# Choosing the tokens of three sequences before the spectra of all eight are done, in a one-core spectral filter with routed experts

## The chip, the cores and the metric

One core of one Trainium2 chip runs the kernel. The metric is device microseconds for one execution. Engines are named as in the profile: PE (TensorE matmuls), PEld (weight loads), DVE (VectorE), ACT (ScalarE), POOL (GpSimd), SP (SyncE, here a queue of transfers).

## The reference

```python
# x (8, 2496, 256); filt_r, filt_i (1249, 256); capacity 80; 8 experts
X = np.fft.rfft(x, axis=1)
y = np.fft.irfft(X * (filt_r + 1j*filt_i)[None], n=2496, axis=1)   # (8, 2496, 256)
t = y.reshape(19968, 256)
logits = t @ w_gate                                   # (19968, 8)
expert_idx = argmax(logits, 1); gate_w = softmax(logits)[expert_idx]
out = 0
for e in range(8):                                    # 80 tokens of the largest gate_w each
    tok = the 80 tokens of expert e with the largest gate_w
    out[tok] = gate_w[tok, None] * (relu(t[tok] @ w1[e]) @ w2[e])
```

Only 640 of 19,968 rows of the filtered sequence are needed, but which ones is known only when all logits are.

## The kernel before

**Forward part.** The transform is split into 39 x 64 points. The work of sequence `b` is in 10 units `u`; a step `v` (line 482) takes unit `v`, `v = 10 b + u`, and issues, in an order written out by hand: `stage2` (PE tile `pb`, then two DVE multiplications by the filter, line 306, and two POOL additions, line 312), `transpose1` of unit `v+2` (tile `pt`), one or two `stage1` matmul groups of a later sequence (tile `pa`; they run out at step 67), and `turn` of unit `v-2` (tile `py`: the spectrum turned back and multiplied by the gate's columns; ACT copies the spectrum, line 333, DVE adds the gate part to `z`, lines 336 and 340). `pb`, `pt` and `pa` share the four one-bank buffers of the PSUM pool `fps`. Spectra 0 and 1 stay in SBUF, the others are stored to `yf` from ACT's queue.

**Logits and gating.** `logits` and the six parts of `gating` (softmax, best expert, each sequence's eight best candidates per row of 128) follow in the steps of the next pair of sequences; those of the last pair, 6 and 7, come after step 81 (lines 513 to 516).

**Choice.** `pick` (line 539) is a chain on DVE with small matmuls between: merge candidates (547, 549), ten rounds of maximum and replace over 256 values for the 80th best of each expert (563, 565), broadcast it (573), mark and count what is kept (580 to 591), pack codes (594 to 613), and two sets of one-hot matrices (628, 654) whose matmuls (633, 659) give the list of positions `idxb` of each sequence and the tokens of each expert.

**Back part.** Eight tiles, one a sequence (`back`, line 698): POOL gathers 128 rows of a cosine table by `idxb` (706), PE transposes them in five groups of four (715), DVE and ACT copy (718), 20 matmuls with the sequence's spectrum add up 128 filtered rows (721), which SP stores to `y_sel` (726).

**Branch and experts.** Line 759 reads a flag on every engine; were it set (a limit of the choice overrun), a general path would redo the choice. Then eight experts: gather 80 rows (785), transpose (795), two layers (802, 816), scatter (820). From the branch on, and in `pick` and `back`, the framework's scheduler orders the instructions; the forward part is in program order. The loads of zeros into `out`, spectra and weights are on SP's queue.

Of the kernel before, what the change touches and what calls it, by code (L numbers as in the profile page):

```python
# [10 lines left out]
AL = mybir.AluOpType  # L11
# [70 lines left out]
def kernel(  # L82
# [98 lines left out]
    NY = 2  # L181
    yf = {b: dpool.tile([128, NS, C], F32, name=f"yf_{b}") for b in range(NY, B)}
# [4 lines left out]
    ZR = S // 4  # L187
    zero_t = zp.tile([128, ZR * C // 128], F32, name="zero_t")
    zeros = list(range(4 * B))
# [8 lines left out]

    zs = [consts.tile([128, E, SP], F32, name=f"z_{i}") for i in range(2)]
# [3 lines left out]
    with ExitStack() as fctx:  # L203
        def pool(name, bufs, space=None):
            kw = {} if space is None else {"space": space}
            return fctx.enter_context(tc.tile_pool(name=name, bufs=bufs, **kw))

        tpool = pool("tables", 1)
# [3 lines left out]
        t2pool = pool("t2", 5)  # L212
        fspool = pool("fs", 3)
        ppool = pool("pp", 2)
        gpool = pool("gp", 1)
        fps = pool("fps", 4, PSUM)
        yps = pool("yps", 2, PSUM)

# [27 lines left out]
        def turn_filter(v, k):  # L246
            f = fst[:, v]
            ps = fps.tile([128, 2, NDB, 128], F32, name=f"pf_{k}_{v}", tag="f")
# [8 lines left out]
        def load_x(b, ch):  # L257
            xt = xpool.tile([NJ * N1, JC, C], F32, name=f"x_{b}_{ch}", tag="x")
            ng = min(JC, NG - JC * ch)
            nc.sync.dma_start(  # L260
                out=xt[:, 0:ng, :],
                in_=bass.AP(tensor=x.tensor, offset=x.offset + (b * S + JC * ch) * C,
                            ap=[[N2 * C, N1], [(NG - 1) * C, NJ], [C, ng], [1, C]]))
            st["x", b, ch] = xt

        def stage1(b, k):
# [4 lines left out]
            for i in range(2):  # L271
                for cb in range(NDB):
                    nc.tensor.matmul(  # L273
                        out=ps[:, i, :, 2 * NS * cb:2 * NS * cb + 2 * NS],
                        lhsT=xt[:, (2 * k + i) % JC, 128 * cb:128 * cb + 128],
# [40 lines left out]
        def turn(b, u):  # L316
# [17 lines left out]
            if b >= NY and u % 2 == 1:  # L334
                nc.scalar.dma_start(out=yf[b][:, 2 * u - 2:2 * u + 2, :], in_=st["ys"])
# [6 lines left out]
        def logits(b, part):  # L342
            if part == 0:
# [3 lines left out]
                ps = fps.tile([128, 2, 2, N2], F32, name=f"pv_{b}", tag="f")  # L347
# [6 lines left out]
            else:  # L354
                p, v = b // 2, st.pop(("v", b // 2))
                ps = fps.tile([128, 2, N1, 4], F32, name=f"pl_{p}", tag="f")
# [9 lines left out]
        def gating(p, part):  # L366
# [45 lines left out]
            elif part == 4:  # L412
                pk = fps.tile([128, 4, 2, N2], F32, name=f"pk_{p}", tag="f")
# [5 lines left out]
            else:  # L419
                for i in range(2):  # L420
# [6 lines left out]
                    scalar=16.0, in1=cbase[:, 2 * p:2 * p + 2, :], op0=AL.mult, op1=AL.add)  # L427

        LATE, LEAD = 2, 2
        with tc.manual_schedule():  # L430
# [50 lines left out]
            load_d(4)  # L481
            for v in range(B * NU + LATE):
                b, u = divmod(v, NU)
                if b < B:
# [16 lines left out]
                    if b > 0 and u in (2, 4, 6, 8):  # L501
                        put_zeros(1)
# [9 lines left out]
            assert not (xs or s1)  # L512
# [5 lines left out]
    wpool = ctx.enter_context(tc.tile_pool(name="weights", bufs=2))  # L518
    w1s, w2s = {}, {}

    def load_weights(e, wpool=wpool):
        w1s[e] = wpool.tile([128, NDB, FF], F32, name=f"w1_{e}", tag="w1")
        nc.sync.dma_start(out=w1s[e], in_=moe_w1[e].rearrange("(k p) f -> p k f", p=128))
        w2s[e] = wpool.tile([128, NFC, C], F32, name=f"w2_{e}", tag="w2")
        nc.sync.dma_start(out=w2s[e], in_=moe_w2[e].rearrange("(k p) d -> p k d", p=128))

    idxs = consts.tile([cap, E], I32, name="idxs")
    idxg = consts.tile([cap, E], I32, name="idxg")
    gate = consts.tile([cap, E], F32, name="gate")
    idxt = consts.tile([cap, E], I32, name="idxt")  # L530
    idxb = consts.tile([128, B], I32, name="idxb")
    more = consts.tile([1, 1], I32, name="more")
    nof = consts.tile([cap, E], F32, name="nof")
    ohb = consts.tile([cap, E, B], F32, name="ohb")
    bad = consts.tile([1, 1], I32, name="bad")
    y_sel = dpool.tile([128 * (B + NX), C], F32, name="y_sel")
    rows = rows_dram.ap()

    def pick(sp, pp):
        f_t = sp.tile([128, 4, KR], F32, name="f_t")  # L540
        off_e = sp.tile([128, 1], F32, name="off_e")

        row = sp.tile([128, KR], F32, name="row")
        rest = sp.tile([128, B * KC], F32, name="rest")
        cf = cand[:].rearrange("p b k -> p (b k)")
        for i in range(KR // 8):
            nc.vector.max(out=row[:, 8 * i:8 * i + 8], in_=cf if i == 0 else rest[:])
            if i + 1 < KR // 8:
                nc.vector.match_replace(out=rest[:], in_to_replace=row[:, 8 * i:8 * i + 8],
                                        in_values=cf if i == 0 else rest[:], imm_value=-1.0)  # L550
        spread = sp.tile([128, 16, KR], F32, name="spread")
        nc.vector.tensor_tensor(
            out=spread[:], in0=row[:].unsqueeze(1).to_broadcast([128, 16, KR]),
            in1=thot[:].unsqueeze(2).to_broadcast([128, 16, KR]), op=AL.mult)
        pall = pp.tile([E, 16 * KR], F32, name="pall")
# [684 lines left out]
```

## Time and profile before

| | us |
|---|---|
| three runs, median (lowest, highest) | 515.06 (513.83, 516.34) |
| the profiled execution, its own time | 514.17 |
| its span, first to last instruction | 512.3 |
| PE busy, share of the span | 441.4, 86% |
| DVE, ACT, POOL busy | 208.2, 204.0, 175.9 |
| mean granted TensorE clock | 0.925 of full speed |

A row of the page or of an answer gives an engine, the line of the kernel, the operation, `out<-in`, the sizes and times. Busy time tells little by itself here: the span falls into stages, and what ends the wait in a stage is read from that stage's rows.

### The profile page before, as it was taken

To read this page: it belongs to the slowest core of one execution; us is meant where nothing else is said; L and a number is where in the kernel's file an instruction comes from. 1 tells how busy PE (TensorE), PEld (TensorE's weight loads), DVE (VectorE), ACT (ScalarE), POOL (GpSimd) and SP (SyncE) were. 2 spreads that over 40 slices of the span, in tenths; PEclk is the share of its full clock that TensorE was granted. 3 is DMA by queue.
4 is the path that set the end of the run, shared out by engine and by line. 5 is a ranking of instruction groups with operands and counts; after the bars stand their busy time and mean duration, and the time that the engine had idled before them with its cause. 6 is when DMAs were issued, how large, how long until landed. Compare 5 with 4: busy or idle time off the path is not lost. (4 is left out here: it accounts for less than half of the span.)

```text
span 512.3 us, 8535 instructions
## 1 busy us (share of the span) xinstructions
PE 441.4 (86%) x3341; PEld 413.0 (81%) x3341; DVE 208.2 (41%) x552; ACT 204.0 (40%) x307; POOL 175.9 (34%) x244
## 2 busy tenths in 40 slices
PE   5789999999999999999999610299999992799993
PEld 5779999999999999999999500288888881788882
DVE  2145444448644477444697478312221110001110
ACT  4756766667666667766655210001100000001110
POOL 7586443434534335344356301520010002112111
PEclk9999999999999999999999955589999997569998
DMA  7999445458677676799223498533589913925830
GB/s 220 253 276 345 139 124 177 144 170 265 213 260 252 204 236 210 231 366 377 84 85 124 149 391 323 206 103 124 166 354 368 354 42 127 355 63 175 275 96 13
DMA packets 32849, 108.09 MB, mean 211 GB/s; under 512 B 3778, under 2 KB 13826, under 8 KB 31010
## 3 DMA queue, kind: packets, MB, share of 16 engines
q1 hardware_dynamic: 24656, 76.93, 45.5%
q0 software_dynamic: 3408, 14.74, 8.4%
q10 hardware_dynamic: 4738, 15.80, 7.8%
q8 instruction: 29, 0.48, 0.4%
q14 instruction: 18, 0.15, 0.1%
HBM read 68.97 MB, written 38.48 MB: 210 GB/s over the span
## 5 line engine op out<-in xcount | busy, mean ns | idle before, releaser
L312 POOL TENSOR_TENSOR p<-p,p 128x256 f32<-128x256 f32 x160 | 113.9, 733 | 133.1 <-DVE p L306 88.4
L306 DVE TENSOR_TENSOR p<-pb,ft 128x512 f32<-128x512 f32 x160 | 102.2, 680 | 9.8 <-PE pb L298 9.8
L273 PE MATMUL pa<-wf_t,x 117*128 117x120 f32 x704 | 91.9, 278 | 6.8 <-DMA x<-in_x_dram 6.8
L279 ACT COPY t<-pa 128x480 f32<-128x480 f32 x88 | 86.8, 1002 | 24.7 <-PE pa L273 24.4
L273 PEld LDWEIGHTS pa<-wf_t,x 117*128 117x128 f32 x704 | 86.0, 195 | 7.1 <-DMA x<-in_x_dram 5.4
L321 PE MATMUL py<-gi,p 128*128 128x136 f32 x640 | 88.1, 280 | 0.8 <-POOL p L312 0.8
L298 PE MATMUL pb<-d_t,t 128*128 128x128 f32 x640 | 84.4, 275 | 0.0
L321 PEld LDWEIGHTS py<-gi,p 128*128 128x128 f32 x640 | 79.8, 190 | 1.4 <-POOL p L312 1.4
L298 PEld LDWEIGHTS pb<-d_t,t 128*128 128x128 f32 x640 | 78.1, 192 | 0.0
L289 ACT COPY t<-pt 128x512 f32<-128x512 f32 x80 | 46.8, 585 | 63.8 <-PE pt L287 63.8
L336 DVE COPY z<-py 128x16 f32<-128x16 f32 x80 | 14.9, 186 | 100.9 <-ACT ysp L333 66.8
L721 PE MATMUL pr<-yb,wt 128*128 128x256 f32 x240 | 53.8, 379 | 0.0
L718 ACT COPY wt<-pw 128x512 f32<-128x512 f32 x16 | 9.4, 586 | 108.6 <-PE pw L715 108.6
L721 PEld LDWEIGHTS pr<-yb,wt 128*128 128x128 f32 x240 | 44.7, 190 | 5.6
L287 PE MATMUL pt<-ident,t 128*128 128x128 f32 x320 | 48.0, 273 | 0.0
L333 ACT COPY ysp<-py 128x512 f32<-128x512 f32 x60 | 35.3, 588 | 8.2 <-PE py L321 8.2
L287 PEld LDWEIGHTS pt<-ident,t 128*128 128x128 f32 x320 | 37.7, 141 | 0.0
L802 PEld LDWEIGHTS ph<-xs,w 128*128 128x128 f32 x256 | 36.1, 227 | 1.1 <-DVE xs L798 0.5
L802 PE MATMUL ph<-xs,w 128*128 128x80 f32 x256 | 36.1, 311 | 0.3 <-DVE xs L798 0.3
L715 PE MATMUL pw<-ident,gt 128*128 128x128 f32 x160 | 24.4, 297 | 11.3 <-DMA gt<-rows_tbl,idxb 8.5
L715 PEld LDWEIGHTS pw<-ident,gt 128*128 128x128 f32 x160 | 19.4, 151 | 16.7 <-issue 8.8
L816 PE MATMUL po<-w,hT 128*80 128x256 f32 x128 | 31.1, 393 | 0.0
(161 smaller groups left out, 299.5 us busy)
## 6 DMA issues: line engine op xcount, KB each, us to landing
out_dram<-zero_t SPq DMA_DIRECT2D x32, 624.0 KB
x<-in_x_dram SPq DMA_DIRECT2D x40, 468.0 KB
w<-in_moe_w_dram SPq DMA_DIRECT2D x16, 1024.0 KB
yf<-ysp ACTq DMA_DIRECT2D x30, 512.0 KB
yb<-yf SPq DMA_DIRECT2D x6, 2560.0 KB
x<-in_x_dram SPq DMA_DIRECT2D x8, 234.0 KB
d_t<-d_tbl SPq DMA_DIRECT2D x5, 256.0 KB
y_sel<-yr SPq DMA_DIRECT2D x8, 128.0 KB
```

Of the source, the lines that this page charges most:

```text
L273: nc.tensor.matmul(out=ps[:, i, :, 2 * NS * cb:2 * NS * cb + 2 * NS], lhsT=xt[:, (2 * k + i) % JC, 128 * cb:128 * cb + 128], rhs=wf_t[:], ...
L279: nc.scalar.copy(out=t1[:, 2 * k - h:2 * k - h + 2], in_=ps[:])
L287: nc.tensor.transpose(ps[:, i, cb, :], t1[:, a:a + 2, :].rearrange("p r n -> p (r n)"), ident[:])
L289: nc.scalar.copy(out=t2[:].rearrange("p i c -> p (i c)"), in_=ps[:].rearrange("p i c q -> p (i c q)"))
L298: nc.tensor.matmul(out=ps[:, cb, i], rhs=d_t[:, 2 * u + i, :], start=True, stop=True, lhsT=t2[:, i, 128 * cb:128 * cb + 128])
L306: nc.vector.tensor_tensor(out=pt, in0=ps[:].rearrange("p c s r q -> p (c s) r q"), in1=f.unsqueeze(2).to_broadcast([128, 2 * NDB, 2, NQ]), ...
L312: nc.gpsimd.tensor_tensor(out=yt[:, :, r, :], in0=yt[:, :, r, :], in1=pr[1][:, :, 1 - r, :], op=op)
L321: nc.tensor.matmul(out=ps[:, i, ZW * cb:ZW * cb + ZW], rhs=gi[:, cb, :], lhsT=yt[:, 2 * cb + i].rearrange("p r q -> p (r q)"), start=True, ...
L333: nc.scalar.copy(out=dst, in_=ps[:, :, E:E + C])
L715: nc.tensor.transpose(ps[:, i, :], gt[:, 128 * s:128 * s + 128], ident[:])
L721: nc.tensor.matmul(po[:], lhsT=wts[s // SG][:, s % SG, :], rhs=yb[:, s, :], start=(start and s == 0), stop=(stop and s == NS - 1))
L802: nc.tensor.matmul(ph[:, fc // 4, fc % 4, 0:cap], lhsT=w1s[e][:, k, 128 * fc:128 * fc + 128], rhs=xs[:, k, :], start=(k == 0), stop=(k == ...
```

## The change

1. **Early choice.** In steps 67 to 77 a first choice runs over the candidates of sequences 0 to 5 that are known by then. It finds for each expert a lower bound of the final threshold (the 80th best of 128 values, found from the other end by stripping the 48 smallest in six rounds), keeps what lies above it in sequences 0 to 2, and writes their `idxb`; `fetch(0)` and `fetch(1)` gather their table rows on POOL in steps 76 and 77. The gating parts of pair 4 and 5 are drawn together into steps 64 to 67 for it.
2. **Three tiles beside the end.** The back tiles of sequences 0 to 2 are cut into pieces (`turn_rows`: four transposes and an ACT copy; `add_rows`: four of the 20 matmuls) and put by hand between the matmuls of the last logits, gating and final choice, which gives `idxb` of sequences 3 to 7 and the tokens of all experts. All of it, tiles and experts included, is now in program order.
3. **PSUM and SBUF.** `fps` has three buffers (four before); one new bank `pkps` takes the filter transposes, logits, gating and choice. `t2` has four buffers (five before). All eight spectra are stored to `yf` (ten more transfers of 512 KB), zeros go out as 64 transfers of half the size, one a step.
4. **General path at the end.** The flag is read, and the branch taken or not, after the experts; the general path has experts of its own. While the flag is set, the experts before it write nothing.

```diff
-        t2pool = pool("t2", 5)
-        fps = pool("fps", 4, PSUM)
+        t2pool = pool("t2", 4)
+        sp = pool("pick", 1)
+        fps = pool("fps", 3, PSUM)
         yps = pool("yps", 2, PSUM)
+        pkps = pool("pkps", 1, PSUM)
...
+            early = {67: [lambda: pick_edge(0, 6, 8, -1.0)],
+                     68: [lambda: pick_all(0, 8)],
+                     70: [lambda: pick_least(0, 8 * n0 - 1, -1.0)],
+                     71: [lambda: pick_tau(0), lambda: pick_kept(0, 0, NE)],
+                     72: [lambda: pick_sums(0, 0, NE), lambda: pick_codes(0, 0, NE)],
+                     73: [lambda: pick_fields(0), lambda: pick_rows(0, 0, NE, 0),
+                          lambda: pick_rows(0, 0, NE, 1), lambda: pick_full(0, 0, NE)],
+                     74: [lambda: pick_rows(0, 0, NE, 2), lambda: pick_rows(0, 0, NE, 3)],
+                     75: [lambda: pick_rows(0, 0, NE, 4)],
+                     76: [lambda: pick_rows(0, 0, NE, 5), lambda: pick_rows(0, 0, NE, 6),
+                          lambda: fetch(0)],
+                     77: [lambda: fetch(1)]}
...
-                    if b > 0 and u in (2, 4, 6, 8):
+                    if b > 0:
                         put_zeros(1)
...
-                    if u in (4, 5, 6, 7, 8, 9):
+                    if b < 6 and u in (4, 5, 6, 7, 8, 9):
                         gating(b // 2 - 1, u - 4)
+                    elif b == 6 and u in (4, 5):
+                        gating(2, 2 * u - 8)
+                        gating(2, 2 * u - 7)
+                    elif b == 6 and u in (6, 7):
+                        gating(2, u - 2)
+                for act in early.pop(v, []):
+                    act()
+                if v >= B * NU:
+                    turn_rows(0, v - B * NU)
...
+            go(1)
             logits(B - 1, 0)
+            go(1)
             logits(B - 1, 1)
-            for part in range(6):
+            for part in range(4):
                 gating(NP - 1, part)
+            go(4)
+            gating(NP - 1, 4)
+            gating(NP - 1, 5)
+            bctx.close()
...
+            spectrum(2)
+            go(3)
+            pick_edge(1, B, KR, 1.0)
+            pick_all(1, KR)
+            for i in range(ntop):
+                pick_top(1, i, ntop, 16 * KR)
+            go(8)
+            fetch(2)
+            pick_least(1, cap - 1, 1.0)
+            pick_tau(1)
+            pick_kept(1, 0, B)
+            go(1)
+            pick_sums(1, NE, B)
+            pick_codes(1, NE, B)
+            pick_full(1, NE, B)
+            pick_bad()
+            pick_fields(1)
+            pick_slots(1)
+            for part in range(5):
+                pick_rows(1, NE, B, part)
+            pick_slots(0)
+            go(2)
+            pick_rows(1, NE, B, 5)
+            pick_rows(1, NE, B, 6)
+            for t in range(NE, 6):
+                fetch(t)
+            go(1)
+            pick_slots(2)
+            go(next(i for i, w in enumerate(work) if w[1] == NE))
+            go(len(work))
+            ex = Experts(nc, cap, ident, fp, ...)
...
+            ex.layer1(0)
+            for e in range(E):
+                if e + 3 < E:
+                    ex.gather(e + 3)
+                if e + 1 < E:
+                    ex.layer1(e + 1)
+                ex.layer2(e)
```

`go(n)` issues the next `n` pieces of the tiles, in the order add 0, turn 2, add 1, turn 3 and so on.

PE at the end of the forward part, from the last `pb` on. Before:

```order
L298 MATMUL pb_9_3184<-d_t,t_7_9_3152 128x128 x4
L321 MATMUL py_7_3195<-gi,p_7_7_3141 128x136 x4
L321 MATMUL py_8_3204<-gi,p_7_8_3168 128x136 x4
L321 MATMUL py_9_3213<-gi,p_7_9_3189 128x136 x4
L349 MATMUL pv_3222<-e_t,z_132 128x128 x2
L359 MATMUL pl_3226<-wi_t,v_3021 128x156 x4
L415 MATMUL pk_3250<-ident,key 128x128 x3
L556 MATMUL pall<-spread,ehot 8x256
```

With the change, from the last but one `py` on (`pw`: transposes of a tile's rows, `po`: its sums, `pv` and `pl`: logits):

```order
L355 MATMUL py_8_3361<-gi,p_7_8_3326 128x136 x4
L487 MATMUL pw_0_3370<-ident,gts_3287 128x128 x4
L355 MATMUL py_9_3377<-gi,p_7_9_3346 128x136 x4
L487 MATMUL pw_1_3386<-ident,gts_3287 128x128 x4
L498 MATMUL po_3392<-ys_467,wt_0_3375 128x256 x4
L385 MATMUL pv_3397<-e_t,z_146 128x128 x2
L487 MATMUL pw_2_3401<-ident,gts_3287 128x128 x4
L395 MATMUL pl_3408<-wi_t,v_3121 128x156 x4
L498 MATMUL po_3392<-ys_467,wt_0_3375 128x256 x4
L487 MATMUL pw_3_3436<-ident,gts_3287 128x128 x4
L498 MATMUL po_3392<-ys_467,wt_2_3406 128x256 x4
L487 MATMUL pw_4_3446<-ident,gts_3287 128x128 x4
```

Pieces of tile 0 stand between the last steps and the logits; the first, `pw_0`, stands ahead of the last `py` and needs the gathered rows.

DVE in step 73 of the changed kernel, up to the first multiplication of step 74 (the `p` rows are the filter products, `z` the gate sums, the rest is early choice; before, the step has the first four rows alone):

```order
L340 TENSOR_TENSOR p_7_3_3141<-pb_3_3136,ft_189 128x512
L340 TENSOR_TENSOR p_7_3_3143<-pb_3_3136,ft_190 128x512
L371 COPY z_146<-py_1_3155 128x2x8
L375 TENSOR_TENSOR z_146<-z_146,py_1_3155 128x2x8
L601 CAST ci_3164<-ccode_3132 128x16
L604 TENSOR_SCALAR fi_3166<-ci_3164 128x16 x4
L607 CAST f_t_3171<-fi_3166 128x64
L613 TENSOR_TENSOR bhot_3173<-f_t_3171,iota 128x16x3
L618 TENSOR_TENSOR bval_3175<-bhot_3173,f_t_3171 128x16x3 x2
L624 TENSOR_TENSOR bplc_3178<-f_t_3171,iota 128x512
L645 TENSOR_SCALAR viol<-rcnt_3088 128x1
L648 TENSOR_SCALAR vb_3181,viol<-misc_3083 128x3
```

Twelve instructions now stand ahead of the next step's multiplication, eight of them new (those with x2 and x4 counted once).

PE in the third expert. Before, two of the preceding expert's second-layer matmuls stand between the transpose `px` and the first layer `ph` that needs its copy:

```order
L795 MATMUL px_7409<-ident,xg_7366 128x80 x2
L816 MATMUL po_7434<-w_1_3981,hT_7390 80x256 x2
L802 MATMUL ph_7414<-xs_7412,w_2_7325 128x80 x16
L816 MATMUL po_7434<-w_1_3981,hT_7390 80x256 x6
L795 MATMUL px_7450<-ident,xg_7407 128x80 x2
```

With the change:

```order
L1015 MATMUL px_4200<-ident,xg_4112 128x80 x2
L1022 MATMUL ph_4205<-xs_4203,w_3994 128x80 x16
L1037 MATMUL po_4225<-w_3934,hT_4176 80x256 x8
L1015 MATMUL px_4246<-ident,xg_4150 128x80 x2
L1022 MATMUL ph_4251<-xs_4249,w_4116 128x80 x16
```

Nothing stands between `px` and `ph` any more.

## Rows read from the trace of the kernel before

**Rows 1.** Stages, windows view: start:end, us, busy PE, PEld, DVE, ACT, POOL; clock, DMA

```profile
15.00:289.00 274.00, 268.33 (x2353) 265.00 (x2352) 152.76 (x379) 178.24 (x264) 133.23 (x185) 1.00 0.65 214
289.00:331.00 42.00, 7.08 (x58) 5.02 (x58) 25.97 (x101) 2.25 (x4) 8.85 (x11) 0.54 0.75 282
...
426.00:438.30 12.30, 0.00 (x0) 0.03 (x1) 0.30 (x1) 0.00 (x0) 2.72 (x3) 0.61 0.64 205
```

**Rows 2.** Timeline, end of the forward part to the first tile: start, us, engine, instruction

```profile
287.87 1.19 PE L321 MATMUL py<-gi,p 128*128 128x136 f32 x8 [0.62 <-POOL p L312]
...
303.47 0.42 DVE L563 MAX8 top<-pall 8x8 f32<-8x256 f32 x1 [1.15 <-PE pall L556]
...
312.75 0.58 PE L573 MATMUL misc<-edge,ehot_t 8*128 8x1 f32 x2 [9.32 <-DVE edge L568]
...
323.80 1.05 POOL L706 DMA_INDIRECT gt<-rows_tbl,idxb  x1 [3.06 <-issue]
...
330.89 3.85 PE L715 MATMUL pw<-ident,gt 128*128 128x128 f32 x16 [8.50 <-DMA gt<-rows_tbl,idxb]
```

**Rows 3.** Timeline, PE in the third back tile and the start of the fourth

```profile
356.14 1.04 PE L715 MATMUL pw<-ident,gt 128*128 128x128 f32 x8
...
359.52 8.37 PE L721 MATMUL pr<-yb,wt 128*128 128x256 f32 x38
...
367.73 0.49 PE L715 MATMUL pw<-ident,gt 128*128 128x128 f32 x3
```

**Rows 4.** Windows view, where the granted clock fell and rose

```profile
292.00:293.00 1.00, 1.00 (x6) 0.62 (x4) 0.00 (x0) 0.00 (x0) 0.00 (x0) 0.61 0.00 0
...
336.00:337.00 1.00, 1.00 (x6) 0.92 (x5) 0.52 (x1) 0.00 (x0) 0.28 (x1) 0.71 0.00 0
```

**Rows 5.** Timeline, PE and DVE in two plain forward steps

```profile
153.62 1.05 PE L298 MATMUL pb<-d_t,t 128*128 128x128 f32 x8
...
154.75 1.27 DVE L306 TENSOR_TENSOR p<-pb,ft 128x512 f32<-128x512 f32 x2
...
156.76 1.05 PE L298 MATMUL pb<-d_t,t 128*128 128x128 f32 x8
```

**Rows 6.** Timeline, DVE and PE in steps with gating, then two saturated DVE steps

```profile
250.32 1.28 DVE L306 TENSOR_TENSOR p<-pb,ft 128x512 f32<-128x512 f32 x2
...
251.44 1.05 PE L298 MATMUL pb<-d_t,t 128*128 128x128 f32 x8
...
266.38 1.28 DVE L306 TENSOR_TENSOR p<-pb,ft 128x512 f32<-128x512 f32 x2
...
267.88 1.28 DVE L306 TENSOR_TENSOR p<-pb,ft 128x512 f32<-128x512 f32 x2
```

**Rows 7.** One line each: durations in ns min/median/max, first and last start

```profile
L403 DVE TENSOR_TENSOR sh<-first,fm x4: 419/746/757, 124.7 to 296.5; 128x312 f32<-128x312 f32 x4
...
L405 DVE TENSOR_TENSOR key<-sh,gwr x4: 482/892/893, 125.5 to 297.0; 128x312 f32<-128x312 f32 x4
...
L628 DVE TENSOR_TENSOR bplc<-f_t,iota x2: 1421/1424/1428, 318.2 to 320.4; 128x1024 bf16<-128x1024 f32 x2
```

**Rows 8.** Timeline, from the last back tile to the first expert

```profile
425.88 0.42 DVE L725 COPY yr<-pr 128x256 f32<-128x256 f32 x1 [7.51 <-PE pr L721]
...
430.57 0.91 POOL L785 DMA_INDIRECT xg<-y_sel,idxg  x1 [34.91 <-DVEq L760]
...
438.30 0.77 PE L795 MATMUL px<-ident,xg 80*128 80x80 f32 x4 [12.46 <-DMA xg<-y_sel,idxg]
```

**Rows 9.** Timeline, PE in the fourth expert

```profile
465.15 0.30 PE L795 MATMUL px<-ident,xg 80*128 80x80 f32 x2
...
466.16 3.69 PE L802 MATMUL ph<-xs,w 128*128 128x80 f32 x32
```

**Rows 10.** The end: last scatter (timeline), and the closing line's drains

```profile
505.25 0.91 POOL L820 DMA_INDIRECT out_dram<-ys,idxs  x1 [2.54 <-ACT ys L819]
...
L1235 POOLq DRAIN  x3: 46/109/6125, 505.0 to 511.7; - x3
```

More of the change, by code (lines that the diff above doesn't have):

```diff
@@ L178 @@
     nc.gpsimd.memset(ones_bf[:], 1.0)
-    NY = 2
-    yf = {b: dpool.tile([128, NS, C], F32, name=f"yf_{b}") for b in range(NY, B)}
+    NE, NY = 3, 2
+    yf = {b: dpool.tile([128, NS, C], F32, name=f"yf_{b}") for b in range(B)}
     ypool = ctx.enter_context(tc.tile_pool(name="spec", bufs=NY))
@@ L186 @@
     zp = ctx.enter_context(tc.tile_pool(name="zero", bufs=1))
[L187 removed]
+    ZR = S // 8
     zero_t = zp.tile([128, ZR * C // 128], F32, name="zero_t")
[L189 removed]
+    zeros = list(range(8 * B))
     def put_zeros(n):
@@ new lines, in spectrum, with weights, turn_rows @@
+        def spectrum(t):
+            p = ypool if t % NE < NE - 1 else st["yx"]
+            ybs[t] = p.tile([128, NS, C], F32, name=f"yb_{t}", tag="ys")
+            nc.sync.dma_start(out=ybs[t], in_=yf[t])
+        def weights(e, p, tag):
+            load_weights(e, p.tile([128, 2 * NFC * C], F32, name=f"w_{e}", tag=tag))
+        def turn_rows(t, g):
+            ps = fps.tile([128, SG, 128], F32, name=f"pw_{t}_{g}", tag="f")
+            for i in range(SG):
+                s = SG * g + i
+                nc.tensor.transpose(ps[:, i, :], gts[t // 2][:, t % 2, 128 * s:128 * s + 128],
+                                    ident[:])
+            if g % 2 == 0:
+                wts[t, g // 2] = xpool.tile([128, 2, SG, 128], F32, name=f"wt_{t}_{g}", tag="x")
+            nc.scalar.copy(out=wts[t, g // 2][:, g % 2], in_=ps[:])
@@ new lines, in add_rows @@
+        def add_rows(t, g):
+            if g == 0:
+                pos[t] = yps.tile([128, 2, 512], F32, name=f"po_{t}", tag="y")
+            for i in range(SG):
+                s = SG * g + i
+                nc.tensor.matmul(pos[t][:, 0, 0:C], lhsT=wts[t, g // 2][:, g % 2, i, :],
+                                 rhs=ybs[t][:, s, :], start=(s == 0), stop=(s == NS - 1))
+            if g == NS // SG - 1:
+                yr = t2pool.tile([128, 2, C], F32, name=f"yr_{t}", tag="t2")
+                nc.scalar.copy(out=yr[:, 0, :], in_=pos[t][:, 0, 0:C])
+                nc.scalar.dma_start(out=y_sel[128 * t:128 * t + 128, :], in_=yr[:, 0, :])
@@ new lines @@
+                if v >= B * NU:
+                    turn_rows(0, v - B * NU)
+            assert not (xs or s1 or early)
+            put_zeros(len(zeros))
+            for t in range(NY):
+                ybs[t] = ysb[t]
+            work = []
+            for t0, t1 in ((0, NE), (NE, B)):
+                order = [("t", t, g) for t in range(t0, t1) for g in range(NS // SG)]
+                work += order[:2]
+                for n, (_, t, g) in enumerate(order):
+                    work.append(("m", t, g))
+                    work += order[n + 2:n + 3]
@@ L698, in back @@
+            for e in range(3):
+                ex.gather(e)
+            weights(3, st["yx"], "ys")
+            weights(4, ypool, "ys")
+            weights(5, t1pool, "t1")
+            ex.layer1(0)
+            for e in range(E):
+                if e + 3 < E:
[3 more added lines that the diff above has]
+                ex.layer2(e)
+                if e + 6 < E:
+                    weights(e + 6, wpool, "w")
     def back(mp, mps, nm, loads, put, idx, start=True, stop=True, acc=None, pad=False):
@@ L800, in layer1 @@
+        nc.vector.tensor_copy(out=xs[:], in_=px[:, 0:NDB, 0:cap])
+        ph = self.banks(f"ph{nm}_{e}").rearrange("p i (j t) -> p i j t", j=4)
         for fc in range(NFC):
```

588 lines of the change are left out of this document (335 added, 253 removed).

## Prediction

> **What bounds the kernel now.** I read the stages first, then the timeline at their seams, then single lines. Until 289 us PE is the bound: 268.33 us busy of 274.00 [rows 1]; the last `py` starts at 287.87 and ends at 289.06 [rows 2]. From there to 331 PE is busy for 7.08 us of 42.00 [rows 1]: the logits and gating, then a DVE chain, ten rounds from 303.47 to the threshold's matmul at 312.75, the first gather at 323.80, the first tile at 330.89 [rows 2]. Then eight tiles; one period is 356.14 to 367.73, 11.59 us [rows 3]. After the last tile PE stands still from about 425.9 to 438.30 [rows 8]. The granted clock falls to half about 3.2 us after the last `py`, while PE does a few logits matmuls (0.61 on the mean of 292 to 293), and is back at full about 2 us after the first 256-column matmuls of the first tile (0.71 in 336 to 337) [rows 4]; in 426 to 438.3 it falls again (0.61) [rows 1]. So 42 us of PE's time lie between two stages that PE bounds, and the change puts three tiles there. The profiled execution took 514.2 us, 0.9 below the median of 515.06, with 1.9 outside its span; the sum is made against 514.2.
>
> **The stretch of the final choice: -31 us.** Now it takes from 289.06 to the fourth tile's start at 367.73, 78.7 us [rows 2, 3]. With the change PE's matmuls in it are three tiles of some 10.7 us (20 transposes at 0.43 per four, 40 passes at 0.215 [rows 3]), 32, and about 5 for logits, transposes of keys and the choice's small matmuls (most of the 7.08 [rows 1], at full clock). The first half is covered: four pieces (4.3 us) beside 4.5 us of gating, eight (8.5 us) beside the ten rounds' 9.3 [rows 2]. The second is not. From the threshold at 312.75 to the `idxb` ahead of the gather at 323.80 [rows 2] the chain takes 11 us, and lasts about as long in program order. PE has a turn, then waits for the matmul of the flag, which stands ahead of the next two pieces (2.1 us): some 7.5 us stand open. If the clock falls in it, as it did before, the next pieces run at half speed (sixteen turns in 3.85 us at 330.89, eight in 1.04 at 356.14 [rows 2, 3]); for a piece or two of 2.1 us that is 2.5 us more. In all 32 + 5 + 7.5 + 2.5 = 47, so 78.7 - 47 = -31 (bounds -36 if gap and clock cost nothing, -26 if both are twice as dear). Next in line is the gather of tile 3: issued 2 us later in the chain and 7.1 us on its way (323.80 to 330.89 [rows 2]), it lands about 3 us before PE gets there.
>
> **Tiles 3 to 7: -3.** With turns two pieces ahead, the waits for copies go: 11.59 to between 10.7 and 11.6, taken at 11.0, times five (bounds -4.5 and 0). Table gathers and spectra are fetched one tile ahead or more; ACT does all five copies of a tile.
>
> **The forward steps: +16.** This is the price. With three banks and three tiles a step, the next `pb` takes the bank of this one and waits for both DVE multiplications. In a plain step there is room: they end at 156.02, the next `pb` comes at 156.76 [rows 5]. In the double steps the extra `pa` takes the bank instead and waits about 0.2, seven times: 1. In a step with gating there is no room: the multiplications begin at 250.32 and end at 251.60, the next `pb` stood at 251.44 [rows 6]. Following a gating's six steps in order, each delay of `pb` moving the `z` behind it, PE loses 0.2, 0.7, 1.0, 1.4, 1.4 and 2.5 us in total: 2.5 for each of two pairs, 5. In steps 64 to 76 the third gating comes closer and the early choice is added. DVE needs 1.5 us a step when it never waits (266.38 to 267.88 [rows 6]), 19.5; gating 6.5; the choice about 12 (25.97 us of DVE in 289 to 331 [rows 1], less gating, with half-width rounds and three of eight sequences). That is 38 us, where PE needs 3.15 a step to step 67 [rows 5] and 2.26 from there, 33; and DVE cannot work ahead, as each `z` waits for that step's ACT copy, some 4 us more. Walking the steps, `pb` comes 3.5 us later in step 69, 5.5 in 73, 7 in 76, 8.4 in 77. POOL then has two gathers of about 1 us ahead of its additions; the first leaves at about 290 and lands 7.1 us later, and the first turn of tile 0, for which it is fetched, stands ahead of the last `py`: 9.7 late in all. So 1 + 5 + 9.7 = 16. Bounds: 3 (only the choice's matmuls and the gather count, DVE catching up in its slack) and 23.
>
> A page speaks against the early choice. Two gating lines with both inputs in SBUF took 419 and 482 ns at the least, 746 and 892 at the median, the least ones with POOL idle [rows 7]. The Trainium skill, "SBUF — State Buffer", section "Who interferes with whom", says that a DVE instruction with two SBUF inputs contends with a GpSimd instruction that reads SBUF, and that whichever issues second is blocked until the other is through; these rows agree. The early choice has seven such operations in steps 73 to 75, four of them `bplc` halves (1424 ns whole [rows 7], so about 0.7 each). Were each blocked by a POOL addition, 0.7 each, the steps would lose 5 us more; I take none in the sum, as POOL is also idle in part, and keep it as a rival.
>
> **The seam to the experts: -3.** Now 425.88 to 438.30, with the gather issued at 430.57 behind the branch [rows 8]. Without the branch it follows the store directly, about 1 to 2 us earlier, and five of the weight loads that crowd it go out before (bounds -4 and 0). PE still idles there for some 9 us, and I keep the half clock at the start of the experts as it is.
>
> **The experts: +4.** At present two second-layer matmuls cover the copy between `px` at 465.15 and `ph` at 466.16 [rows 9]. Now PE waits: `px` 0.30, DVE's copy 0.32, two handovers, 0.6 seven times (bounds 0 and 4.5).
>
> **The end: +2.** The last scatter is issued at 505.25 and the drain lasts 6.1 us [rows 10]; a flag load, a branch and its rendezvous come behind it now, which at their present place cost 1 to 2 us after the store (bounds 0 and 5).
>
> **The rest: +0.5.** The ten added stores are ACT's to issue, with ACT busy for 178.24 of 274 us, and DMA at 0.65 [rows 1]; double zeros of half the size ride beside. If transfers were short of room, SP's loads of `x`, a sequence ahead, would hide it (bounds 0 and 2).
>
> **Sum:** -31 - 3 + 16 - 3 + 4 + 2 + 0.5 = -14.5: 514.2 - 14.5 = 499.7 us.
>
> **The rivals.** *Main case*, as summed, its own range 492 to 507: 0.50. *DVE catches up* (0.24): the forward part loses 4 us instead of 16, giving 488; DVE is busy for only 152.76 of 274 us [rows 1] in its favour, and against it that the work falls in 13 steps, where a late multiplication stops PE at once. *Blocked by POOL* (0.12): with the 5 us above, 505. *PE stays at half clock* (0.06), the one on the other side: its place is the gap after the threshold. Should the mixture of turns and sums not bring back full clock, a tile costs about twice its 10.7 us, as the turns at 330.89 did against those at 356.14 [rows 2, 3]. From the second such tile on the gain of 14.5 us is gone, and tiles 2 to 7 together, 64 us more, would give about 560. For it: the clock fell in both gaps [rows 1, 4]. Against: it rose at 336.6 in just such a mixture [rows 4], and forward steps, a quarter of them transposes, ran at 1.00. *The change does not do what it says, or the steps cost far more* (0.08): if the early choice keeps more than 128 tokens of a sequence, or the lists overrun, the flag sends everything through the general path, some twice the time. The reference's inputs put through the same rule keep 113, 102 and 109 of sequences 0 to 2, so this part is small; the greater part is the upper bounds met together, 23 us in the steps and 5 at the end, 510 to 520.
>
> **How the numbers follow.** A measurement of this kernel can tell about 0.5% from no change, 2.6 us. Faster by more (under 512.5): main, catching up and blocked, 0.50 + 0.24 + 0.12 = 0.86, less 0.02 for their tails: 0.84. Same 0.07 and slower 0.09 share the rest. The range: up from 499.7 by the forward bound (+7), the dear end and gap, 511; down by the catching up and the low bounds of stretch and tiles, 485.
>
> **What would show it.** Right: `pb` waiting on DVE in steps 65 to 77, the last `py` near 305; PE busy in most of the next 47 us; tile 3 at about 352, tiles of 11 us, `px` to `ph` at 0.7 us in later experts, one more rendezvous at the end. Wrong: forward steps at the old pace, PE at 1.2 GHz through the tiles, weights late in the experts, or instructions of the general path.

## The result: 3.1% faster, and the profile after

| | before | changed |
|---|---|---|
| median of four runs each, us | 515.70 | 498.98 |
| lowest to highest | 513.83 to 518.22 | 498.16 to 503.17 |
| profiled execution, its span | 514.2, 512.3 | 498.2, 496.4 |
| mean granted clock | 0.925 | 0.956 |

Ratio 0.969, 95% interval 0.962 to 0.976. The forecast was 499.7. Medians and ratios, here and below, leave out three single runs that stand apart: one of the kernel before at 1189 us, whose cause no record shows, one of the filled gap at 500.3 and one of the run with all edits at 480.8. The forecast's terms, stretch by stretch, from the two profiled executions:

| stretch, us | before | changed | difference | forecast |
|---|---|---|---|---|
| start to the end of the last `py` | 289.1 | 300.3 | +11.2 | +16 |
| to the end of tile 2's sums | 78.7 | 45.2 | -33.5 | -31 |
| tiles 3 to 7, to the last sum | 58.2 | 56.0 | -2.2 | -3 |
| to the first `px` | 12.4 | 12.1 | -0.3 | -3 |
| to the last scatter | 66.9 | 72.0 | +5.0 | +4 |
| to the end | 7.1 | 10.7 | +3.7 | +2 |

The windows view of the changed kernel has these stretches (columns as in [rows 1]) and two short ones where the clock was down:

```profile
15.00:300.30 285.30, 273.94 (x2379) 269.89 (x2378) 164.03 (x429) 179.04 (x266) 135.96 (x186) 0.99 0.69 226
300.30:345.50 45.20, 38.80 (x235) 32.80 (x233) 27.49 (x105) 11.21 (x20) 6.64 (x9) 0.96 0.80 314
345.50:401.50 56.00, 54.68 (x301) 47.61 (x299) 0.00 (x0) 16.30 (x30) 9.71 (x11) 1.00 1.00 375
401.50:413.70 12.20, 0.06 (x2) 0.04 (x1) 0.00 (x0) 0.37 (x1) 3.78 (x4) 0.62 0.94 344
413.70:485.70 72.00, 67.03 (x400) 56.44 (x400) 6.44 (x16) 7.25 (x16) 10.49 (x12) 0.87 0.22 74
288.00:292.00 4.00, 3.58 (x21) 3.59 (x22) 3.64 (x10) 0.51 (x1) 3.09 (x4) 0.57 0.00 0
333.00:337.00 4.00, 4.00 (x37) 3.33 (x36) 2.00 (x5) 0.00 (x0) 1.32 (x2) 0.60 0.98 413
```

In the second row PE is busy for 38.80 of 45.20 us, where it had 7.08 of 42.00 [rows 1]. In the fourth it stands still with the DMA engines full; in [rows 1] it stood still with them at 0.64. In the fifth the clock is 0.87 on the mean.

Of the 11.2 us of the forward part 10.3 are lost from step 64 on (until then the steps are 0.98 late). PE's timeline there shows the waits:

```profile
256.56 0.55 PE L451 MATMUL pk<-ident,key 128*128 128x128 f32 x3 [0.73 <-DVE key L441]
...
263.75 0.39 PE L527 MATMUL pall<-spread,ehot 128*8 128x128 f32 x2 [1.24 <-DVE spread L519]
...
271.84 0.38 PE L548 MATMUL misc<-edge,ehot_t 8*128 8x1 f32 x2 [0.74 <-DVE edge L543]
...
285.25 1.19 PE L355 MATMUL py<-gi,p 128*128 128x136 f32 x8 [1.34 <-POOL p L346]
...
288.42 0.27 PE L631 MATMUL misc<-bval,bplc 128*128 128x6 bf16 x4 [1.69 <-DVE bplc L624]
288.55 2.05 PE L332 MATMUL pb<-d_t,t 128*128 128x128 f32 x8
...
298.72 0.66 PE L487 MATMUL pw<-ident,gts 128*128 128x128 f32 x4 [1.05 <-DMA gts<-rows_tbl,idxb]
```

No idle time ahead of a `pb` is put down to DVE. What waits are the small matmuls of gating and choice that stand ahead of a `pb` in PE's order (0.73, 1.24, 0.74, 1.69), a `py` for POOL (1.34) and the first turn for its rows (1.05). After the last DVE wait `pb` takes 2.05 us instead of 1.05: the clock has fallen to half (1.2 of 2.4 GHz) already inside the forward part, for some 4 us (288 to 292, above). The six waits sum to 6.8 us and the half clock adds some 1.7; the rest of the 10.3 is not taken apart, and no run leaves out the early choice alone.

In the choice two waits stand open, and the pieces behind the second run at half clock (a `po` piece 3.38 us instead of 1.89):

```profile
327.76 0.16 PE L667 MATMUL misc<-vsum,ones_bf 128*128 128x1 bf16 x1 [2.28 <-DVE vsum L666]
...
332.88 0.57 PE L631 MATMUL misc<-bval,bplc 128*128 128x10 bf16 x16 [2.68 <-DVE off_e L678]
333.31 3.38 PE L498 MATMUL po<-yb,wt 128*128 128x256 f32 x8
```

At the seam between the last tile and the experts, timelines of SP, ACT, POOL and PE (the four engines' rows in order of time; SP's durations are those of the issuing):

```profile
384.24 6.12 SPq L217 DMA_DIRECT2D w<-in_moe_w_dram  x1
...
401.05 1.16 SPq L219 DMA_DIRECT2D w<-in_moe_w_dram  x1
...
401.99 0.33 ACTq L503 DMA_DIRECT2D y_sel<-yr  x1
...
408.88 0.94 POOL L1004 DMA_INDIRECT xg<-y_sel,idxg  x1 [36.90 <-DMA w<-in_moe_w_dram]
...
413.69 0.50 PE L1015 MATMUL px<-ident,xg 80*128 80x80 f32 x2 [12.14 <-issue]
414.66 7.11 PE L1022 MATMUL ph<-xs,w 128*128 128x80 f32 x32 [0.47 <-DVE xs L1018]
```

The last store is issued 0.4 us after the last sum; the gather that needs it follows 6.9 us later. Ahead of the store SP had issued six loads of 1 MB (experts 3 to 5), the first at 384.24 and the last at 401.05. (In the program this gather waits for the stores to `y_sel` and for no load of weights; the releaser in its row is inferred by the profile.) The first `ph` takes 7.11 us at half clock, a later one 3.80. In a later expert and at the end, PE and POOL:

```profile
442.15 0.30 PE L1015 MATMUL px<-ident,xg 80*128 80x80 f32 x2
442.87 3.80 PE L1022 MATMUL ph<-xs,w 128*128 128x80 f32 x32 [0.42 <-DVE xs L1018]
446.51 3.62 PE L1037 MATMUL po<-w,hT 128*80 128x256 f32 x16
449.96 0.30 PE L1015 MATMUL px<-ident,xg 80*128 80x80 f32 x2
...
485.66 0.91 POOL L1042 DMA_INDIRECT out_dram<-ys,idxs  x1 [2.54 <-ACT ys L1040]
```

### The profile page after: what moved, and what is told of

Its sections match the earlier page's. It is cut to its first block, busy times and chain, and to the rows that moved or that the text cites. A ratio compares the mean times of both kernels' runs of the same rounds, so it can differ in the third digit from the quotient of the medians.

```text
span 496.4 us, 8607 instructions
## 1 busy us (share of the span) xinstructions
PE 443.9 (89%) x3363; PEld 416.1 (84%) x3363; DVE 201.1 (41%) x574; ACT 220.9 (45%) x339; POOL 176.4 (36%) x244
## 5 line engine op out<-in xcount | busy, mean ns | idle before, releaser
L307 PE MATMUL pa<-wf_t,x 117*128 117x120 f32 x704 | 93.3, 281 | 5.7 <-DMA x<-in_x_dram 5.7
L307 PEld LDWEIGHTS pa<-wf_t,x 117*128 117x128 f32 x704 | 87.7, 198 | 5.7 <-DMA x<-in_x_dram 5.7
L332 PE MATMUL pb<-d_t,t 128*128 128x128 f32 x640 | 86.5, 279 | 2.1 <-remote 2.1
L332 PEld LDWEIGHTS pb<-d_t,t 128*128 128x128 f32 x640 | 79.2, 194 | 2.6 <-remote 2.2
L498 PE MATMUL po<-yb,wt 128*128 128x256 f32 x240 | 58.1, 387 | 1.3 <-ACT wt L491 1.3
L498 PEld LDWEIGHTS po<-yb,wt 128*128 128x128 f32 x240 | 44.4, 195 | 6.9 <-ACT wt L491 1.8
L491 ACT COPY wt<-pw 128x512 f32<-128x512 f32 x40 | 23.2, 586 | 55.2 <-PE pw L487 50.7
L1018 DVE COPY xs<-px 128x160 f32<-128x160 f32 x8 | 2.6, 324 | 91.4 <-PE px L1015 91.4
L1037 PE MATMUL po<-w,hT 128*80 128x256 f32 x128 | 29.6, 387 | 0.0
L1042 POOL DMA_INDIRECT out_dram<-ys,idxs x8 | 7.5, 934 | 60.4 <-ACT ys L1040 60.4
```

Source lines behind the costliest of these rows:

```text
L307: nc.tensor.matmul(out=ps[:, i, :, 2 * NS * cb:2 * NS * cb + 2 * NS], lhsT=xt[0:NJ * N1, (2 * k + i) % JC, 128 * cb:128 * cb + 128], rhs=w ...
L332: nc.tensor.matmul(out=ps[:, cb, i], rhs=d_t[:, 2 * u + i, :], start=True, stop=True, lhsT=t2[:, i, 128 * cb:128 * cb + 128])
L498: nc.tensor.matmul(pos[t][:, 0, 0:C], lhsT=wts[t, g // 2][:, g % 2, i, :], rhs=ybs[t][:, s, :], start=(s == 0), stop=(s == NS - 1))
L1037: nc.tensor.matmul(po[0:cap, :], lhsT=hT[:, fc, :], rhs=self.w2s[e][:, fc, :], start=(fc == 0), stop=(fc == NFC - 1))
```

## The experiments

Steps before 64 end between 242.1 and 248.3 us in profiles of kernels that are the same up to there, so that runs are compared by stretches, not by their spans. Each edit is made in the changed kernel; a ratio is that to the kernel before, timed beside it (medians 512.2 to 515.4 us). "Choice" is the stretch from the last `py` to the end of tile 2's sums (45.2), "seam" from the last sum to the first `px` (12.1), "experts" from there to the last scatter (72.0).

**Everything behind the choice.** All `go(n)` up to `pick_slots(2)` are taken out; the last two issue what is left.

> All pieces of tiles 0 to 2 are issued behind the final choice, with everything else as in the changed kernel: the early choice is paid for, and its tiles stand beside nothing. Theory (the tiles fill PE's idle time in the chain of the final choice, and the chain does not get longer for them: it takes 34.8 us from the last py to the positions with the tiles and 34.7 before): some 32 us of PE's work come behind positions at 335, so that tile 3 starts at 367 to 369 instead of 345.5, the whole 520 to 524. Rival (the chain is drawn out by the pieces between its matmuls): the positions come earlier than 333 here and the loss is under 18 us.

Measured 524.1 us, ratio 1.017 (1.013 to 1.021). The positions are written 34.8 us after the last `py`, with the pieces between it was 34.6. (By the same row of DVE, the one that writes `idxb`, the kernel before took 33.8; the 34.7 of the expectation is to its first gather.) The pieces then take 34.4 us by themselves:

```profile
300.20:335.00 34.80, 5.91 (x45) 3.79 (x43) 25.53 (x93) 2.84 (x5) 3.63 (x6) 0.62 0.41 162
335.00:369.40 34.40, 34.40 (x190) 30.23 (x191) 1.94 (x13) 8.35 (x16) 3.01 (x3) 0.94 0.70 256
```

So the tiles cost the chain nothing on balance, and standing beside it is worth 23.9 us of this stretch (69.2 against 45.2). PE stood idle for 28.9 of the chain's 34.8 us; the pieces fill 23.9 of them, and the 5.0 that stay are about the two open waits of the choice (2.28 and 2.68). The balance has two sides: with the pieces the last logits (`pl`) start 0.8 us later, 3.1 us behind the last `py` instead of 2.3, and the chain's own matmuls then run faster, as the clock is up (`pall` 0.59 us instead of 1.01, `pk` 0.52 instead of 0.87). Without the pieces beside the chain the change is 1.7% slower than before: the early choice and the new order are paid, and only the 2 us of tiles 3 to 7 are got for them.

**Cover for the copy.** `layer1` is split, and the `px` of the expert after next goes ahead of `layer2`:

```diff
-                if e + 1 < E:
-                    ex.layer1(e + 1)
+                if 0 < e < E - 2:
+                    ex.turn(e + 2)
                 ex.layer2(e)
+                if e + 2 < E:
+                    ex.layer1(e + 2)
```

> In the changed kernel PE waits about 0.42 us in each expert between px and ph for DVE's copy, and px starts 7.81 us after the px before it, where the kernel before had 7.13. Here px of the expert after next is issued ahead of the second-layer matmuls, so that these stand between every px and its ph. Theory (the missing cover is the term 'experts'): px to px falls to 7.2 to 7.3 us, the experts take 3.5 to 5 us less, the whole some 494.5 instead of 499. Rival (the weights or the outputs set the pace): the period stays at 7.8, PE waiting for weights instead, time unchanged.

Measured 492.7 us, ratio 0.960 (0.956 to 0.964); experts 69.0 us, 3.0 less. From the third expert on no wait is left in PE's rows, and `px` follows `px` after 7.12 us:

```profile
436.37 0.30 PE L1022 MATMUL px<-ident,xg 80*128 80x80 f32 x2
436.51 3.62 PE L1049 MATMUL po<-w,hT 128*80 128x256 f32 x16
439.96 3.69 PE L1034 MATMUL ph<-xs,w 128*128 128x80 f32 x32
443.49 0.30 PE L1022 MATMUL px<-ident,xg 80*128 80x80 f32 x2
```

The period fell as expected; the whole stretch gave a little less (3.5 to 5 expected): five periods of 0.69 make 3.4, and some 0.4 is lost in the first experts, where the first `po` takes 5.74 us instead of 4.47, more of it at half clock.

**Weights held back.** A copy into each weight buffer makes its load wait for the third expert's gathered rows:

```diff
-            weights(3, st["yx"], "ys")
-            weights(4, ypool, "ys")
-            weights(5, t1pool, "t1")
+            weights(3, st["yx"], "ys", ex.xg[2][0:1, 0:8])
+            weights(4, ypool, "ys", ex.xg[2][0:1, 0:8])
+            weights(5, t1pool, "t1", ex.xg[2][0:1, 0:8])
```

> In the changed kernel SP issues the weights of experts 3 to 5 from 384 to 401 us, and the last tile's store, issued at 402.0, is followed by the first expert's gather only at 408.9. Here these three loads wait for the third expert's gathered rows. Theory (the store stands behind 6 MB of weights on the DMA engines): the first gather is issued some 2.5 us after the store instead of 6.9, the first px comes 4 to 5 us earlier, the whole about 495. Rival (the store and the gather take that long by themselves): the first px stays 11 to 12 us behind the last sum, time unchanged; or the later weights come too late and PE waits ahead of the fourth expert's ph, time longer.

Measured 489.6 us, ratio 0.956 (0.952 to 0.960). Store, gather and `px`:

```profile
397.75 0.33 ACTq L506 DMA_DIRECT2D y_sel<-yr  x1
...
400.48 0.95 POOL L1007 DMA_INDIRECT xg<-y_sel,idxg  x1 [26.15 <-issue]
...
403.07 0.50 PE L1018 MATMUL px<-ident,xg 80*128 80x80 f32 x2 [5.76 <-issue]
```

The gather follows the store after 2.7 us (6.9), `px` the gather after 2.6 (4.8): the seam is 5.8 us, 6.4 less, and no later `ph` waits for weights. Theory held, its gain was larger, as the gather too had stood behind weights.

**The gap filled.** 100 transposes of the identity, whose result nobody reads, behind the last sum.

> In the changed kernel PE stands still from 401.6 to 413.7 us and then runs the first two experts' first layers at half clock (7.1 us each instead of 3.8). Here 100 transposes without use, some 10.9 us, fill the gap. Theory (the gap brings the clock down, and work of any kind keeps it up): the granted clock stays at 1.00 and the experts' start saves 7 to 8 us, the whole about 491.5. Rival (the clock falls for another reason, such as the small tiles of the experts, or weights arrive too late to feed full speed): 0 to 2 us.

Measured 491.3 us, ratio 0.961 (0.954 to 0.968); experts 67.6 us, 4.3 less. The windows view from the filling to the second expert's layers:

```profile
398.20:409.30 11.10, 11.00 (x101) 10.76 (x99) 0.00 (x0) 0.37 (x1) 3.38 (x4) 1.00 1.05 386
409.30:412.00 2.70, 0.69 (x5) 0.57 (x6) 0.32 (x1) 0.00 (x0) 0.40 (x1) 1.00 0.48 140
412.00:415.60 3.60, 3.58 (x33) 3.41 (x32) 0.00 (x0) 0.08 (x1) 0.00 (x0) 1.00 0.02 8
415.60:416.80 1.20, 0.00 (x0) 0.02 (x1) 0.72 (x2) 0.36 (x1) 0.00 (x0) 1.00 0.00 0
416.80:427.00 10.20, 10.19 (x48) 8.90 (x49) 0.49 (x1) 0.44 (x1) 0.00 (x0) 0.67 0.01 2
```

The clock stays up through the gap and the first expert, and falls in the second, after PE had been idle for 2.0 of 2.7 and for 1.2 us. Half of the theory: work without use holds the clock, but what is left idle behind it loses it again. The Trainium skill, "TensorE: Matmul & The Clock Gate", Part 1, says that the slow clock is the default and activity releases it; these rows agree, and show that the activity need not be useful.

**Pieces into the choice's gap.** The flag's sum (`pick_bad`) moves behind the lists, and `go(6)` stands ahead of their matmul.

> In the changed kernel PE waits 2.28 us for the flag's sum and 2.68 us for the position lists of tiles 3 to 7, and the piece behind runs at half clock. Here six pieces in one go stand ahead of the lists' matmul, the flag's sum comes behind the lists, so the lists come about 1 us earlier as well. Theory (the open gap of the choice): PE has no wait over 1 us between the threshold and the lists, and the third tile's last sum ends 4 to 5 us earlier; tile 3's rows, gathered 7 us after the lists, arrive at 341 to 342 and then set the start of tile 3, so 3 to 4 us come off, the whole about 495.5. Rival (the gather is late anyhow, or the five tiles behind are bound by transfers): 0 to 1 us.

Measured 495.6 us, ratio 0.968 (0.963 to 0.972); the choice took 44.8 us, tiles 3 to 7 55.0. A miss, with its reason in PE's rows:

```profile
332.27 0.16 PE L667 MATMUL misc<-vsum,ones_bf 128*128 128x1 bf16 x1 [3.10 <-DVE vsum L666]
332.29 3.76 PE L498 MATMUL po<-yb,wt 128*128 128x256 f32 x8
```

The lists came 2.0 us earlier and PE met no wait ahead of them, but now it waited 3.10 us for the flag behind them and ran at half clock for 5.7 us (332.3 to 338). The gap was moved, not closed.

**The early lists behind `pb`.** Their matmul follows step 77's `pb`, both gathers are issued in step 77, and the first two turns follow the first logits.

> In the changed kernel the matmul of the early lists stands ahead of pb of step 77 and waits 1.69 us for the last bplc, the clock falls to half for some 4 us, and the first turn of tile 0 waits 1.05 us for its rows ahead of the last py. Here the early lists' matmul follows pb of step 77 (its positions stay ahead of that step's multiplications), and the first two turns come behind the first logits. Theory (PE's order, not DVE's work, costs the last 2 to 3 us of the forward part): the clock stays up, the last py ends at 297 to 298 instead of 300.3, the whole about 496.5. Rival (DVE's work and the gather of tile 0 set the end): the last py comes earlier but PE waits as much ahead of the first tile, time unchanged within 1 us.

Measured 501.5 us, ratio 0.975 (0.971 to 0.980): no gain; the last `py` ends at 300.6, the choice took 45.5. The wait went elsewhere:

```profile
298.04 1.19 PE L357 MATMUL py<-gi,p 128*128 128x136 f32 x8 [2.79 <-POOL p L348]
```

Two gathers in a row on POOL now stand ahead of its additions. The rival's result, by another way than it named; and since several things were moved at once, the run does not say what PE's order alone costs.

**One input of `bplc` in PSUM.** The early halves compare with a copy of `iota` in the bank of `misc`.

> The early choice's four bplc halves compare two SBUF inputs; three of them took 1.19 us beside POOL additions and one 0.68 with POOL idle. Here one of the two inputs lies in PSUM (one ACT copy more). Theory (by the Trainium skill, SBUF — State Buffer, Who interferes with whom, an instruction with a single SBUF input does not contend): each takes 0.7 us, POOL's additions beside them 0.73 instead of 1.17, and the forward part ends 1.5 to 2 us earlier, the whole about 497. Rival (they are slow for another reason, or DVE is not what is waited for there): 1.19 stays, or it falls and the time does not move by 0.5 us.

Measured 499.2 us, ratio 0.968 (0.964 to 0.972). The groups of that line, first of the changed kernel (both choices), then of this one (early choice with `misc`, final with `iota`; ns min/median/max):

```profile
L624 DVE TENSOR_TENSOR bplc<-f_t,iota x8: 677/890/1209, 281.2 to 332.1; 128x512 bf16<-128x512 f32 x8
```

```profile
L629 DVE TENSOR_TENSOR bplc<-f_t,misc x4: 675/679/680, 283.3 to 288.3; 128x512 bf16<-128x512 f32 x4
L629 DVE TENSOR_TENSOR bplc<-f_t,iota x4: 678/784/889, 330.2 to 332.5; 128x512 bf16<-128x512 f32 x4
```

The contention is shown: 1.19 became 0.68 with POOL's additions running beside, and these went from 1.17 back to 0.73. From step 64 to the last `py` the kernel took 52.4 us instead of 54.2, the 1.8 that were expected. But the choice took 46.6, 1.4 more: the clock fell at the first of its two waits instead of the second (a `po` piece of 2.71 us at 328.2) and was back only at about 339. The price of the contention is right, though not all of the 1.8 is contention: the early lists' matmul waited 0.85 us instead of 1.69, and the `pb` behind it took 1.14 instead of 2.05, so the half clock there went as well. Its removal alone is worth nothing that can be measured.

**No general path.** The flag's load, the branch and the general path are left out.

> The general path with the flag's load and branch at the end is left out (it redoes the choice where a limit is overrun, which these inputs do not do). Theory (the branch's end waits for the last scatter, and the closing drain begins only then): the time from the last scatter's issue to the end falls from 10.7 us to the 7 us of the kernel before, the whole about 495.5. Rival (the drain takes what it takes, whenever it begins): 10 us stay.

Measured 496.5 us, ratio 0.963 (0.960 to 0.967); last scatter to end 6.7 us instead of 10.7. The closing drains of the changed kernel and of this one:

```profile
L1441 POOLq DRAIN  x3: 46/103/4970, 490.5 to 496.1; - x3
```

```profile
L1402 POOLq DRAIN  x3: 46/103/6127, 488.0 to 494.6; - x3
```

The long drain begins 4.9 us after the last scatter's issue with the branch, and beside it without: 4.0 us for the branch at this place. Where they go is seen in POOL's queue in the changed kernel, which takes the branch at 486.0 us:

```profile
L956 POOLq EVENT_SEMAPHORE  x5: 17/42/43, 488.7 to 489.0; - x5
L956 POOLq INC_SWDGE_SEM  x1: 1400/1400/1400, 489.1 to 489.1; - x1
```

The last scatter's transfers show on the DMA engines until 488; the queue's next instructions start at 488.7, and one of 1.40 us stands ahead of the drain at 490.5. The ratio agrees: it is 0.006 below the changed kernel's 0.969 and 0.009 below the 0.972 of its second timing, 3 to 4.5 us.

**The three edits at the experts together**, with the next two `px` in the middle of the first two first layers, and 48 transposes.

> Three edits together: the weights of experts 3 to 5 behind the gathers, px of the expert after next ahead of the second layer (the next two px in the middle of the first layers before them, so that PE has no wait there), and 48 transposes without use in the 5.8 us that are left of the gap. One by one the edits took 6.4 us (weights), 3.0 (cover) and 4.3 (filled gap, where the clock still fell in the second expert, after waits of 1.6 and 1.2 us) off their own stretches. Theory (three separate costs, and half clock comes with idle PE): the granted clock stays at 1.00 until the end of the experts, the last sum to the last scatter takes 67 to 69 us instead of 84.1, the whole 15 to 17 us less than the changed kernel, ratio to the kernel before about 0.937. Rival (the three overlap: the second and later experts then wait for the held weights, or the clock falls in the small tiles anyhow): 8 to 11 us less.

Measured 476.2 us, ratio 0.930 (0.925 to 0.934). Last sum to last scatter 64.8 us instead of 84.1, 19.3 less:

```profile
395.60:401.40 5.80, 5.27 (x49) 5.06 (x48) 0.00 (x0) 0.37 (x1) 2.03 (x3) 1.00 0.11 37
401.40:460.40 59.00, 57.48 (x400) 48.83 (x400) 6.05 (x16) 7.64 (x19) 12.23 (x14) 1.00 0.57 199
```

More than the 13.7 of the three one by one: with the waits gone as well the clock stayed at 1.00 to the end, which no single edit reached.

**All of it, and the choice filled**: `misc` for the early `bplc`, `go(6)` ahead of the lists, all other pieces of tiles 0 to 2 and then the flag's sum and 36 transposes behind them.

> As the run with the three edits at the experts, and two more: one input of the early bplc in PSUM (it took 1.8 us off the forward steps and lost 1.4 again in the choice, where the clock was at half for longer), and the final choice with the flag's sum behind the lists, all pieces of tiles 0 to 2 ahead of it and 36 transposes without use after it. Theory (the choice is bound by its own chain and then by tile 3's gather, which lands some 10.3 us after the positions; both gains hold if the clock stays up): the positions come 32.6 us after the last py instead of 34.6, tile 3 starts with its gather 42.5 to 43.5 us after the last py instead of 45, the forward steps keep 1.8 us, together 3 to 4 us less than the run with the three edits. Rival (tiles 3 to 7 are bound by transfers, so what starts earlier waits later): under 1 us less.

Measured 470.7 us, ratio 0.917 (0.912 to 0.922).

```profile
296.50:339.50 43.00, 41.21 (x271) 35.64 (x269) 27.59 (x105) 11.59 (x21) 6.76 (x9) 1.00 0.83 320
```

The positions come 32.6 us after the last `py`, the clock stays at 1.00 in the choice, tile 3's first sum starts 44.1 us after the last `py` (46.1 in the run before), and step 64 to the last `py` takes 52.5 us. By stretches that is some 3.3 us, by the medians 5.5: the gains that were lost in the two single runs hold once the clock is up. It beats both kernels.

**The base, unaltered.**

> The changed kernel again, unaltered, on the same chip as the two runs beside it, as their base. All theories: 0.962 to 0.976 of the kernel before, the same stretches as in its first profile within 1 us each (last sum to last scatter 84.1 us, last py to the end of tile 2's sums 43.8 to 45.3).

Measured 498.2 us, ratio 0.972 (0.967 to 0.976): last sum to last scatter 84.7 us, choice 43.8. So the run with all edits is 27.5 us, 5.5%, below the changed kernel on the same chip.

## Why the prediction was right, and where not

**The stretch (-31, measured -33.5): right.** The pieces fill PE and the chain is no longer for them: 34.6 us to the positions with them, 34.8 without, where its own matmuls ran at half clock. The open gap was put at 7.5 us; the trace shows 5.2 between threshold and positions (0.24, 2.28 and 2.68). The half clock, put at 2.5, took 1.6 (0.60 in 333 to 337). Tile 3 started at 345.5, forecast 352; 4.8 of the 6.5 us between them are the forward part's.

**Tiles 3 to 7 (-3, measured -2.2): right**, 11.2 us a tile instead of 11.0.

**The forward steps (+16, measured +11.2): too dear by 5**, and the step that failed is "the next `pb` takes the bank of this one and waits for both DVE multiplications", which gave 5 us for two gatings. Two rows of the timeline in a gating's step, DVE's multiplications of one step and the next `pb`:

```profile
120.35 1.28 DVE L340 TENSOR_TENSOR p<-pb,ft 128x512 f32<-128x512 f32 x2
...
121.08 1.05 PE L332 MATMUL pb<-d_t,t 128*128 128x128 f32 x8
```

The `pb` starts with the multiplications half done, as it did with four banks. The three banks don't go round in turn. PE's instructions of these steps as the built program has them, with the engine that each waits for:

```
L332 MATMUL pb_6_1351<-d_t,t_2_6_1287 128x128 [waits Activation_49]
L321 MATMUL pt_8_1362<-ident,t_2_706 128x128 [waits DVE_49]
L307 MATMUL pa_9_1369<-wf_t,x_4_930 128x3x40 [waits Activation_49]
L355 MATMUL py_4_1378<-gi,p_2_4_1276 128x136 [waits Pool_49]
L332 MATMUL pb_7_1392<-d_t,t_2_7_1329 128x128 [waits Activation_49]
```

`pb` has a bank that ACT's copy frees, and the wait for DVE lies with the transposes `pt`, a microsecond later in PE's order, where it is over. In other steps it lies with `pa`, in a few with `pb` itself. Two gatings cost 0.1 us each; up to step 64 the loss is 0.98 where 6 were summed. For steps 64 to 81 the sum said 9.7, measured 10.3. The size was right, the mechanism in part: DVE was too full, but PE met that at the choice's own matmuls and not at `pb`, and some 1.7 us of it is half clock (`pb`, `pt` and `py` from 288.55 on), which the prediction expected only behind the last `py`. DVE's instructions were longer by the contention that the prediction kept as a rival (three halves by 0.5 each, POOL's additions twice by 0.45). That rival came true in its mechanism and not in its time: 1.8 us at most where it put 5, and worth nothing alone.

**The seam (-3, measured -0.3): wrong.** The step that failed is "five of the weight loads that crowd it go out before". Before, the branch held SP until 430.0 us; six loads of weights came right behind it and crowded the gather, 7.7 us from its issue to `px` [rows 8]. Now nothing holds SP, and the loads run ahead and crowd the store. The removed branch's gain was given back to a queue: 6.4 us, shown by holding the loads back. The Trainium skill, "DMA: Bandwidth & Descriptors", section "Issuing engines are not separate DMA queues", says that transfers run on the same 16 engines whoever issues them; the store on ACT's queue between SP's loads is a case of it.

**The experts (+4, measured +5.0): right**, a wait of 0.42 us and a period of 7.81 where 7.13 had been; 3.0 of it come back with the cover.

**The end (+2, measured +3.7): under-sized, inside its bounds.** With the branch the drain begins only when the last scatter's transfers are over: 4.0 us by the run without it, where 2 were summed.

**The rivals.** The clock came back in the tiles (1.00 from 345.5 on), so half clock for good did not happen; the steps did not stay at the old pace; the flag was not set. Measured less forecast is -4.8 in the steps and -2.5, +0.8, +2.7, +1.0 and +1.7 in the stretches behind, which nearly cancel, with 0.5 forecast for the rest and not seen apart. That the whole came out within 1 us is luck: the time was closer than its terms.

## What to carry to other kernels

Independent work put by hand into a chain of small steps can fill nearly all of PE's idle time in it, here 23.9 of 28.9 us. What is lost lies where PE's next piece stands behind a wait of the chain: look at each small matmul, and what it waits for, rather than at the tile behind it. Taking away a wait that held a queue lets that queue run ahead, and it lands in front of the next urgent small transfer; hold bulk loads behind the gather that they would delay. Where PE must wait for some microseconds, count the half clock after the gap too, here 7 to 8 us behind a gap of 12; filling the gap without use gave 4.3 of them alone, and the clock held to the end only when the waits behind the gap were gone too.

## Not expected of the hardware

Small DVE instructions with a single input were held up beside POOL's additions as well. The cast of sixteen columns took 676 ns in the early choice and 151 in the final one, with POOL idle. The Trainium skill, "SBUF — State Buffer", section "Who interferes with whom", counts casts among those that can contend; the row agrees:

```profile
L601 DVE CAST ci<-ccode x2: 151/414/676, 278.8 to 328.1; 128x16 int32<-128x16 f32 x2
```

The gather of tile 3 took 9.7 us from its issue to its first use (331.02 to 340.75 us in the run with the three edits at the experts) with the DMA engines at 0.9 to 1.0, where 7.1 us passed before [rows 2]. PE waited for it at the start of tile 3:

```profile
340.75 1.06 PE L490 MATMUL pw<-ident,gts 128*128 128x128 f32 x8 [0.99 <-DMA gts<-rows_tbl,idxb]
```

With the choice filled no such wait is seen, as the transposes without use last until tile 3 starts (339.34 us); whether the gather or they set that start is not shown.
